# Second MoE of a fused attention kernel: GpSimd's part of the middle pass, the first rounding, the pace of the weights' decode and the place of y's first sums are changed

## The chip, the cores and the metric

The kernel runs on one core of one Trainium2 chip. The metric is the device time of one launch in microseconds. Lower is better.

## What is computed

Attention with a cumulative-decay bias over 4 x 8 heads of 576 tokens, then two mixture-like dense layers ("MoE") on the 2304 tokens, all in float32:

```python
x = attention(q, k, v, s)                      # (2304, 512)
h = np.maximum(x @ w_in, 0.0); y = h * h @ w_out          # first MoE, 512 -> 2048 -> 512
h = y @ w_in2; g = h * np.cos(h); out = g @ w_out2        # second MoE, the same sizes
```

The change touches the second MoE alone: `g = h * cos(h)` between two products, and what prepares their operands.

## The kernel before, in words

**Precision.** TensorE multiplies float16 in the second MoE. So that float32 accuracy is kept, every operand is split into a high part (rounded to float16) and a low part (the rest), and each product is three matmuls: high x high, low x high, high x low (PASSES).

**Tiling.** The tokens are cut into five blocks j (four of 512 tokens and a last one of 256), the 2048 hidden columns into 16 chunks f of 128. The order of the work is a list of items, written out in `items`: three passes over the chunks, GROUPS = (0..3), (4..8), (9..15); within a pass, all five blocks; within a block, all chunks of the pass. Items 0 to 19 are the first pass (p = 0), items 20 to 44 the middle pass (p = 1), of which items 40 to 44 are the half-size block. In the last pass (p = 2) chunks 10 to 15 of the four large blocks go two at a time, in "units".

**One item** (the loop from L1660). `m2_g1` is the first product, 12 matmuls into the PSUM tile `hp`. `m2_cos` scales it on ScalarE (`a`, L1437) and, on VectorE, rounds it to a whole number by adding and subtracting MAGIC (`kf`, L1438) and takes the difference (L1439). `m2_sin` is ScalarE's Sin (L1444). `m2_mul` multiplies by h on VectorE (L1450). `m2_high` makes the high part `gh` on ScalarE (L1458), `m2_rest` the low part `gl` (L1465): on GpSimd in the middle pass, on VectorE otherwise. `gh` and `gl` of an item are made during the next item. `m2_g2` is the second product (L1480), issued two items late (G2LAG). After the last chunk of a pass its four accumulators (two in the half-size block) leave PSUM: in the first pass they are written to `part`, in later passes added to it, alternately by VectorE (L1487) and by ScalarE and GpSimd (`os` L1492, L1493). Each engine runs its instructions in the order in which they are written.

**The decode of the weights** runs beside the items. A weight tile comes as raw 64-bit words. `w_clip` (ScalarE, L807) and `w_bits` (VectorE, L813 and L817) turn it into float32; `w_square` (ScalarE, L892) and a matmul (L901) sum its squares; `w_scale` makes a power of two of that (VectorE, L908 to L913, and `group` once for a pass); `w_rest` makes the high part (ScalarE, L840 or L866), `w_lo` the low part (VectorE, L883 or L874). How many tiles have had their bits done behind item i is the number `goal` (L1699). Tiles become ready in twos. For chunks 10 to 15 the first product's weights of two chunks are combined ("split" weights): the first of two makes four sums on VectorE (L855) and three parts, the second two parts.

**The transform of y.** In a unit the two chunks' first products are computed in seven smaller products (`prod`, Strassen-like, L1571) on sums of weights and on sums of y. `t_make` makes the sums of y for a block: its first step loads two tiles `yr` (SP's queue, L1057), then come four subtractions (VectorE, L1517), four high parts (ScalarE, L1520) and four low parts (VectorE, L1523), in six more steps. `t_tick` runs one step; it is called once behind each item from T_FROM on, and twice in each unit. The `yr` buffers (two) are also used for the sums of split weights.

**A unit** writes its products into three PSUM tiles `bank`; `snap` (ScalarE, L1581) and `join` (VectorE, L1585) bring them out into `hs`, and a later product into the same bank waits for its snap or join. Between the products stand the halves of earlier second products (`out_part`). At its end: half a second product, a step of `t_tick`, then `m2_cos` of the two chunks.

Of the kernel before, what the change touches and what calls it, by code (L numbers as in the profile page):

```python
# [13 lines left out]
ACTF = mybir.ActivationFunctionType  # L14
# [9 lines left out]
NF = DFF // 128  # L24
# [5 lines left out]
TINY = 2.0 ** -96  # L30
GROUPS = ((0, 4), (4, 9), (9, 16))
PAIR0 = 10
T_FROM = 36
RAWS = 6
NB2 = 5
LAG = (3, 5)
# [92 lines left out]
def attention_moe_moe_kernel(  # L129
# [1102 lines left out]
    def w_rest(j):  # L1232
        w_hi(j)
        wlow.append(j)
# [30 lines left out]
    def w_step(n):  # L1265

        js = list(range(nw[2], min(nw[2] + n, wlim[0])))
        while wlow:
            w_lo(wlow.pop(0))
            yield  # L1270
        w_squares()
        while wrest:
            w_rest(wrest.pop(0))
        if js:
            w_clip_to(js[-1])
            for _ in zip(*[w_bits(j) for j in js]):
                yield
            for j in js:
                if wq[j][0] == 0:
                    wrest.append(j)  # L1280
                else:
                    wbit.append(j)
            nw[2] += len(js)
# [145 lines left out]
                m += 1  # L1429
        hd2[j, f] = hp  # L1430

    def m2_cos(j, f):
        n = blocks[j][1]
        hp = hd2[j, f]
        a = p2.tile([128, n], F32, tag="a", bufs=2, name="a")
        kf = p2.tile([128, n], F32, tag="kf", bufs=2, name="kf")
        nc.scalar.activation(out=a, in_=hp, func=ACTF.Copy, scale=sm["hsc"][:, j, f:f + 1], bias=0.25)  # L1437
        nc.vector.tensor_scalar(out=kf, in0=a, scalar1=MAGIC, scalar2=MAGIC, op0=ALU.add, op1=ALU.subtract)  # L1438
        nc.vector.tensor_tensor(out=kf, in0=kf, in1=a, op=ALU.subtract)  # L1439
        hd2[j, f] = (hp, a, kf)  # L1440
# [20 lines left out]
    def m2_rest(p, j, f):  # L1461
        n = blocks[j][1]
        a, gh = hd2[j, f]
        gl = p2.tile([128, n], F16, tag="gl", bufs=3, name="gl")
        (nc.gpsimd if p == 1 else nc.vector).tensor_tensor(out=gl, in0=a, in1=gh, op=ALU.subtract)  # L1465
        hd2[j, f] = (gh, gl)

    def m2_g2(p, j, f, pick=None):
        t0, n = blocks[j]
        gh, gl = hd2[j, f]  # L1470
        w = wt[1, f, 1]
        first, last = (f == x for x in (GROUPS[p][0], GROUPS[p][1] - 1))
        sc = sm["osc"][:, p, j:j + 1]
        if first:
            ops.setdefault(j, {})
        for a in range(n // 128) if pick is None else pick:
            if first:
                ops[j][a] = ps2.tile([128, DM], F32, tag=f"o{a}", name=f"o{a}")
            for m, (e, x) in enumerate(PASSES):
                nc.tensor.matmul(  # L1480
                    ops[j][a], (gh, gl)[e][:, a * 128:(a + 1) * 128], w[:, x, :],
                    start=(first and m == 0), stop=(last and m == 2),
                )
            if last:
                st = part[4 * j + a]
                if p and (a % 2 == 0 or j == NB2 - 1):
                    nc.vector.scalar_tensor_tensor(  # L1487
                        out=st, in0=ops[j][a], scalar=sc, in1=st, op0=ALU.mult, op1=ALU.add
                    )
                elif p:  # L1490
                    os = p2.tile([128, DM], F32, tag="os", bufs=2, name="os")
                    nc.scalar.activation(out=os, in_=ops[j][a], func=ACTF.Copy, scale=sc)  # L1492
                    nc.gpsimd.tensor_tensor(out=st, in0=os, in1=st, op=ALU.add)  # L1493
                elif a % 2 == 0:
                    nc.scalar.activation(out=st, in_=ops[j][a], func=ACTF.Copy, scale=sc)
                else:
                    nc.vector.tensor_scalar(out=st, in0=ops[j][a], scalar1=sc, scalar2=None, op0=ALU.mult)
            if f == NF - 1:
                for row, x, m in _pieces(t0 + a * 128, 128):
                    nc.sync.dma_start(out=out[row:row + m, :], in_=part[4 * j + a][x:x + m])  # L1500
# [5 lines left out]
    def t_make(j):  # L1506

        to = [half[4 * (j % 2) + x].bitcast(F16).rearrange("p (e c h) -> p e c h", e=2, c=2) for x in range(4)]
        ysc = sm["ysc"][:, j:j + 1]
        load_ys(j)  # L1510
        yield
        r, q = (yr[j, a] for a in range(2))
        t3 = part[18].rearrange("p (c h) -> p c h", c=2)
        src = (r[:, 0:2], q[:, 2:4], t3, r[:, 2:4])

        def minus(o, x, y):
            nc.vector.tensor_tensor(out=o, in0=x, in1=y, op=ALU.subtract)  # L1517

        def high(x):
            nc.scalar.activation(out=to[x][:, 0], in_=src[x], func=ACTF.Copy, scale=ysc)  # L1520

        def low(x):
            nc.vector.scalar_tensor_tensor(  # L1523
                out=to[x][:, 1], in0=src[x], scalar=ysc, in1=to[x][:, 0], op0=ALU.mult, op1=ALU.subtract
            )

        minus(src[2], q[:, 2:4], q[:, 0:2])
        yield
        high(2)
        minus(src[0], q[:, 0:2], r[:, 0:2])  # L1530
        yield
        high(0)
        low(2)
        minus(src[1], q[:, 2:4], src[0])
        yield
        high(1)
        low(0)
        minus(src[3], r[:, 2:4], src[1])
        yield
        high(3)  # L1540
        low(1)
        yield
        low(3)
        yt[j] = to
# [3 lines left out]
    def t_tick(j):  # L1548

        while now2[0] <= min(j, NB2 - 2):  # L1550
            if next(now2[1], now2) is not now2:
                return
            now2[0] += 1
            now2[1] = t_make(now2[0])
# [8 lines left out]
    def prod(j, f, x, b, start):  # L1563
        m, wx, yx = PROD[x]
        w = pair[f][m]
        if start:
            bank[b] = ps2h.tile([128, 2 * HB], F32, tag="h", bufs=3, name="bank")
        n = 0
        for c in range(2):
            for a, e in PASSES:  # L1570
                nc.tensor.matmul(  # L1571
                    bank[b][:, 0:HB], w[:, a, wx, c * 128:(c + 1) * 128], y_side(j, yx, e, c),
                    start=(start and n == 0), stop=(n == 5), skip_group_check=True,
                )
                n += 1
# [13 lines left out]
    def out_part(x, n):  # L1589
        if x is not None:  # L1590
            k = blocks[x[1]][1] // 128 // 2
            m2_g2(*x, pick=range(n * k, n * k + k))

    def unit(j, f, prev):

        p = len(GROUPS) - 1
        w_need(2 * NF + 2 * f + 4)
        while now2[0] <= j:
            t_tick(j)
        first = fifo.pop(0) if len(fifo) != 2 or prev[0] != "u" else None  # L1600
        second = fifo.pop(0) if len(fifo) > 1 else None
        for m in range(2):
            hd2[j, f + m] = stq[0][0].tile([128, 2 * HB], F32, tag="stg", bufs=4, name="hs")
        old = [prev[1:], (prev[1], prev[2], prev[3] + 1)] if prev[0] == "u" else []
        prod(j, f, 1, 0, True)
        prod(j, f, 2, 1, True)
        snap(j, f, 0, 0, 0)
        join(j, f, 1, 0, 0)
        out_part(first, 0)
        for x in old:  # L1610
            m2_sin(*x[1:])
        if old:
            m2_mul(*old[0])
        else:
            m2_high(*prev[1:])
            m2_rest(*prev[1:])
        prod(j, f, 6, 0, False)
        if old:
            m2_high(*old[0])
            m2_mul(*old[1])  # L1620
        snap(j, f, 0, 1, 0)
        prod(j, f, 7, 2, True)
        out_part(first, 1)
        if old:
            m2_high(*old[1])
            m2_rest(*old[0])
            m2_rest(*old[1])
        prod(j, f, 5, 0, False)
        snap(j, f, 0, 1, 1)
        join(j, f, 2, 1, 1)  # L1630
        out_part(second, 0)
        t_tick(j + 1)
        prod(j, f, 3, 0, False)
        snap(j, f, 0, 0, 1)
        prod(j, f, 4, 2, False)
        join(j, f, 2, 1, 0)
        out_part(second, 1)
        t_tick(j + 1)
        for m in range(2):
            m2_cos(j, f + m)  # L1640
            fifo.append((p, j, f + m))

    def unit_rest(p, j, f):
        fs = (f, f + 1)
# [15 lines left out]
    for i, (kind, p, j, f) in enumerate(items):  # L1660
# [11 lines left out]
        m2_g1(j, f)  # L1672
        if prev and prev[0] == "u":
            unit_rest(*prev[1:])
        m2_cos(j, f)
        if i < G2LAG:
            m2_sin(j, f)
            m2_mul(p, j, f)
# [4 lines left out]
        if i >= QUIET:  # L1683
            w_squares()
            while wrest:
                w_rest(wrest.pop(0))
        if p == 0 and j + 2 < NB2 and f == 3:
            first_y(j + 2)
        if i >= G2LAG:
# [6 lines left out]
            last_y(j + 1)  # L1696
        w_lows()
        k = i + 1 - QUIET
        goal = min(4 * NF, bits0 + int(max(0, min(k, PAUSE)) * P_BITS) + max(0, k - PAUSE - 5))  # L1699
        if i >= QUIET:  # L1700
            _weave(w_step(max(0, goal - nw[2])))
        if i >= G2LAG:
# [66 lines left out]
```

## Time and profile before

| | us |
|---|---|
| three runs: median (lowest, highest) | 983.01 (981.57, 983.53) |
| the profiled execution | 983.83 |
| its span, first to last instruction | 982.0 |
| busy in the span: TensorE / VectorE / ScalarE / GpSimd | 951.3 / 762.3 / 687.9 / 162.2 |

The page gives TensorE (PE) 97% of the span, VectorE (DVE) 78%, ScalarE (ACT) 70%, GpSimd (POOL) 17%. It cuts the span in 40 equal slices; a digit is the busy share in tenths:

```
PE   6999999999999999999999999999999899999998
DVE  6899987778777777777994375888789987787675
POOL 2000012111110111111110032420233331001001
```

The second MoE begins near 598 us, in the 25th slice. A matmul is pipelined: the next one starts before the modelled end of the one before, so the time from start to start is the pace, and a row's duration is longer.

### The profile page before, as it was taken

The numbers are of one execution on the slowest core, as the hardware profiler recorded it, in microseconds if no ns is written. First come the engines' busy times: TensorE is split into PE (matmuls) and PEld (weight loads), VectorE is DVE, ScalarE is ACT, GpSimd is POOL, SyncE is SP. The second block draws the span as 40 slices with busy tenths as digits, with TensorE's granted clock in tenths as the row PEclk, the third lists the DMA queues.
The fourth block names the chain that finished last, engine by engine and source line by source line (L and its number), as shares of the span: only waits on it lengthen the run. The fifth ranks groups of instructions, "written<-read, shape, count | busy, mean of one in ns | idle before, by whom it ended". The sixth has DMA issues, their size and how long they took to land.

```text
span 982.0 us, 20976 instructions
## 1 busy us (share of the span) xinstructions
PE 951.3 (97%) x7472; PEld 755.7 (77%) x7472; DVE 762.3 (78%) x1905; ACT 687.9 (70%) x1669; POOL 162.2 (17%) x251
## 2 busy tenths in 40 slices
PE   6999999999999999999999999999999899999998
PEld 5898899999999999999999995445444345656664
DVE  6899987778777777777994375888789987787675
ACT  6799877778778777776784785677567655565553
POOL 2000012111110111111110032420233331001001
PEclk9999999999999999999999999999999999999999
DMA  8984698658988865587994697200000001121001
GB/s 251 301 279 135 151 221 214 168 139 177 170 187 177 184 177 156 128 160 161 200 227 90 238 323 297 64 2 1 1 1 3 21 22 44 51 77 45 27 18 65
DMA packets 151673, 131.43 MB, mean 134 GB/s; under 512 B 107992, under 2 KB 125728, under 8 KB 151568
## 3 DMA queue, kind: packets, MB, share of 16 engines
q1 hardware_dynamic: 147664, 123.78, 48.7%
q0 software_dynamic: 3904, 6.30, 2.5%
q8 instruction: 59, 0.97, 0.4%
q14 instruction: 46, 0.38, 0.1%
HBM read 89.98 MB, written 15.83 MB: 108 GB/s over the span
## 4 chain that ended last, share of the span: by engine, by line
PE 74%; DVE 10%; DMA 7%; ACT 5%; issue 3%; POOL 1%; SPq 0%; DVEq 0%; ACTq 0%; POOLq 0%
PE y L1017 18%; PE hps L988 18%; PE o L1480 14%; PE hp L1426 9%; DMA rw<-in_w_dram 6%; PE bank L1571 5%; PE qkp L560 5%; PE pvs L687 4%; DVE kf L1439 1%; DVE a L1450 1%; PE xps L742 1%; DVE kf L1438 1%; DVE st L817 1%; DVE wt L874 1%; DVE wt L880 1%
## 5 line engine op out<-in xcount | busy, mean ns | idle before, releaser
L988 PE MATMUL hps<-xh,wt 128*128 128x256 f32 x1152 | 238.6, 290 | 2.2 <-ACT g L999 2.0
L1017 PE MATMUL y<-gh,wt 128*128 128x256 f32 x1152 | 236.4, 289 | 0.0
L988 PEld LDWEIGHTS hps<-xh,wt 128*128 128x128 f32 x1152 | 189.9, 192 | 4.5 <-ACT g L999 3.5
L1017 PEld LDWEIGHTS y<-gh,wt 128*128 128x128 f32 x1152 | 189.0, 191 | 1.0
L1480 PE MATMUL o<-wt,gh 128*128 128x512 f16 x576 | 172.3, 381 | 3.7 <-ACT gh L1458 1.6
L988 PE MATMUL hps<-xl,wt 128*128 128x256 f32 x576 | 163.4, 284 | 0.2 <-DVE xl L759 0.2
L1017 PE MATMUL y<-gl,wt 128*128 128x256 f32 x576 | 163.0, 283 | 0.1
L999 ACT ACTIVATE g<-hps 128x256 f32<-128x256 f32 x144 | 54.6, 379 | 102.2 <-PE hps L988 98.0
L1426 PE MATMUL hp<-yh,wt 128*128 128x512 f16 (+1 forms) x448 | 125.2, 349 | 0.0
L1480 PE MATMUL o<-wt,gl 128*128 128x512 f16 x288 | 109.9, 382 | 3.4 <-POOL gl L1465 3.4
L988 PEld LDWEIGHTS hps<-xl,wt 128*128 128x128 f32 x576 | 110.7, 192 | 0.7 <-DVE xl L759 0.4
L1017 PEld LDWEIGHTS y<-gl,wt 128*128 128x128 f32 x576 | 110.2, 191 | 1.0 <-DVE gl L1007 0.4
L1426 PEld LDWEIGHTS <-wt 128*128 128x128 f16 x672 | 64.2, 98 | 59.6 <-issue 1.0
L1480 PEld LDWEIGHTS <-gh 128*128 128x128 f16 x576 | 56.2, 98 | 59.4 <-issue 3.5
L386 POOL DMA_DIRECT2D k<-ext_d x80 | 41.1, 514 | 322.2 <-ACT g L1000 104.6
L601 ACT ACTIVATE sb<-sb,nb 128x128 f32<-128x128 f32 (+7 forms) x152 | 87.5, 576 | 2.5 <-DVE nb L578 2.0
L1444 ACT ACTIVATE a<-kf 128x512 f32<-128x512 f32 (+1 forms) x80 | 46.7, 585 | 49.9 <-DVE kf L1439 48.9
L1007 DVE TENSOR_TENSOR gl<-g,gh 128x256 fp32r<-128x256 f32 x144 | 60.2, 418 | 27.0 <-ACT gh L1001 14.0
L1426 PE MATMUL hp<-yl,wt 128*128 128x512 f16 (+1 forms) x224 | 78.2, 349 | 0.0
L578 DVE CUSTOM_DVE_ANT_0 sb<-qkp,mask 128x128 f32<-128x128 f32 (+7 forms) x152 | 69.3, 456 | 6.9 <-PE qkp L545 3.6
L642 DVE TENSOR_SCALAR p<-sb 128x384 f16<-128x384 f32 (+3 forms) x120 | 43.2, 360 | 39.5 <-ACT sb L601 21.2
L646 DVE SCALAR_TENSOR_TENSOR p<-sb,p 128x384 f16<-128x384 f32 (+3 forms) x120 | 66.4, 553 | 3.8 <-DVE p L642 0.2
(145 smaller groups left out, 1881.9 us busy)
## 6 DMA issues: line engine op xcount, KB each, us to landing
rw<-in_w_dram SPq DMA_DIRECT2D x64, 512.0 KB
raw<-in_qk_dram SPq DMA_DIRECT2D x48, 352.0 KB
yr<-y_d SPq DMA_DIRECT2D x17, 512.0 KB
raw<-in_qk_dram SPq DMA_DIRECT2D x16, 384.0 KB
v_d<-vt SPq DMA_DIRECT2D x16, 320.0 KB
vb<-v_d SPq DMA_DIRECT2D x32, 160.0 KB
vr<-in_v_dram POOLq DMA_DIRECT2D x15, 320.0 KB, 4.6
y_d<-yst SPq DMA_DIRECT2D x18, 256.0 KB
```

Source lines behind the costliest of these rows:

```text
L560: nc.tensor.matmul(p[0:r, 0:cn], m[0:kk, qo:qo + r], m[0:kk, BT + c0:BT + c0 + cn], start=(kk == 128 and not (two and h % 2)), stop=(kk == ...
L578: nc.vector.tensor_tensor_reduce(out=sb[0:r, c0:c0 + cn], in0=p[0:r, 0:cn], in1=mask[0:r, mo:mo + cn], scale=-0.125, scalar=(3.0e38 if k = ...
L601: nc.scalar.activation(out=sb[0:r, 0:w], in_=sb[0:r, 0:w], func=ACTF.Exp, scale=-1.0, bias=j["nb"], accum_out=z[0:r, ti, x:x + 1],)
L646: nc.vector.scalar_tensor_tensor(out=p[0:r, cw:cw + w], in0=sb[0:r, 0:w], scalar=PSC, in1=p[0:r, 0:w], op0=ALU.mult, op1=ALU.subtract,)
L988: nc.tensor.matmul(hp, w[:, a, c * 128:(c + 1) * 128], (xh, xl)[e][:, c, :], start=(n == 0), stop=(n == 3 * KD - 1),)
L999: nc.scalar.activation(out=g, in_=hp, func=ACTF.Relu)
L1007: nc.vector.tensor_tensor(out=gl, in0=g, in1=gh, op=ALU.subtract)
L1017: nc.tensor.matmul(yps[k][d // 2][:, d % 2, :], w[:, a, d * 128:(d + 1) * 128], (gh, gl)[e], start=(f == 0 and n == 0 and d % 2 == 0), sto ...
L1426: nc.tensor.matmul(hp, chunk_of(w, a, c), (yh, yl)[e][:, c, :], start=(m == 0), stop=(m == 3 * KD - 1),)
L1444: nc.scalar.activation(out=a, in_=kf, func=ACTF.Sin, scale=-6.2831850)
L1480: nc.tensor.matmul(ops[j][a], (gh, gl)[e][:, a * 128:(a + 1) * 128], w[:, x, :], start=(first and m == 0), stop=(last and m == 2),)
L1571: nc.tensor.matmul(bank[b][:, 0:HB], w[:, a, wx, c * 128:(c + 1) * 128], y_side(j, yx, e, c), start=(start and n == 0), stop=(n == 5), ski ...
```

## The change

T_FROM falls from 36 to 20, and a rate LATE_BITS of 0.62 weights per item comes into `goal`: the bits of 14 weights fall behind items 19 to 40, where they fell behind items 22 to 35. At most one split weight is finished per item. In the middle pass, `gl` is made by VectorE; all accumulators leave through VectorE (L1487's form); the first rounding, adding MAGIC, is done by ScalarE as a Copy with a bias, and VectorE does both subtractions in one scalar_tensor_tensor. In a unit that follows a unit, the second step of `t_tick` stands before the fifth of the seven products and not at the end, and `m2_cos` of the two chunks stands before the last half of a second product. A unit that follows an item has one step instead of two. `t3`, a temporary of `t_make`, lies in another tile.

```diff
--- before.py
+++ after.py
@@ -30,7 +30,8 @@
 TINY = 2.0 ** -96
 GROUPS = ((0, 4), (4, 9), (9, 16))
 PAIR0 = 10
-T_FROM = 36
+T_FROM = 20
+LATE_BITS = 0.62
 RAWS = 6
 NB2 = 5
 LAG = (3, 5)
@@ -1269,7 +1270,7 @@
             w_lo(wlow.pop(0))
             yield
         w_squares()
-        while wrest:
+        while wrest and not split(wrest[0]):
             w_rest(wrest.pop(0))
         if js:
             w_clip_to(js[-1])
@@ -1429,12 +1430,19 @@
                 m += 1
         hd2[j, f] = hp
 
-    def m2_cos(j, f):
+    def m2_cos(j, f, p=2):
         n = blocks[j][1]
         hp = hd2[j, f]
         a = p2.tile([128, n], F32, tag="a", bufs=2, name="a")
         kf = p2.tile([128, n], F32, tag="kf", bufs=2, name="kf")
         nc.scalar.activation(out=a, in_=hp, func=ACTF.Copy, scale=sm["hsc"][:, j, f:f + 1], bias=0.25)
+        if p == 1:
+            nc.scalar.activation(out=kf, in_=a, func=ACTF.Copy, bias=MAGIC)
+            nc.vector.scalar_tensor_tensor(
+                out=kf, in0=kf, scalar=MAGIC, in1=a, op0=ALU.subtract, op1=ALU.subtract
+            )
+            hd2[j, f] = (hp, a, kf)
+            return
         nc.vector.tensor_scalar(out=kf, in0=a, scalar1=MAGIC, scalar2=MAGIC, op0=ALU.add, op1=ALU.subtract)
         nc.vector.tensor_tensor(out=kf, in0=kf, in1=a, op=ALU.subtract)
         hd2[j, f] = (hp, a, kf)
@@ -1462,7 +1470,7 @@
         n = blocks[j][1]
         a, gh = hd2[j, f]
         gl = p2.tile([128, n], F16, tag="gl", bufs=3, name="gl")
-        (nc.gpsimd if p == 1 else nc.vector).tensor_tensor(out=gl, in0=a, in1=gh, op=ALU.subtract)
+        nc.vector.tensor_tensor(out=gl, in0=a, in1=gh, op=ALU.subtract)
         hd2[j, f] = (gh, gl)
 
     def m2_g2(p, j, f, pick=None):
@@ -1483,7 +1491,7 @@
                 )
             if last:
                 st = part[4 * j + a]
-                if p and (a % 2 == 0 or j == NB2 - 1):
+                if p == 1 or p and (a % 2 == 0 or j == NB2 - 1):
                     nc.vector.scalar_tensor_tensor(
                         out=st, in0=ops[j][a], scalar=sc, in1=st, op0=ALU.mult, op1=ALU.add
                     )
@@ -1510,7 +1518,7 @@
         load_ys(j)
         yield
         r, q = (yr[j, a] for a in range(2))
-        t3 = part[18].rearrange("p (c h) -> p c h", c=2)
+        t3 = half[8 if j else 4].rearrange("p (c h) -> p c h", c=2)
         src = (r[:, 0:2], q[:, 2:4], t3, r[:, 2:4])
 
         def minus(o, x, y):
@@ -1625,6 +1633,7 @@
             m2_high(*old[1])
             m2_rest(*old[0])
             m2_rest(*old[1])
+            t_tick(j + 1)
         prod(j, f, 5, 0, False)
         snap(j, f, 0, 1, 1)
         join(j, f, 2, 1, 1)
@@ -1634,11 +1643,10 @@
         snap(j, f, 0, 0, 1)
         prod(j, f, 4, 2, False)
         join(j, f, 2, 1, 0)
-        out_part(second, 1)
-        t_tick(j + 1)
         for m in range(2):
             m2_cos(j, f + m)
             fifo.append((p, j, f + m))
+        out_part(second, 1)
 
     def unit_rest(p, j, f):
         fs = (f, f + 1)
@@ -1672,7 +1680,7 @@
         m2_g1(j, f)
         if prev and prev[0] == "u":
             unit_rest(*prev[1:])
-        m2_cos(j, f)
+        m2_cos(j, f, p)
         if i < G2LAG:
             m2_sin(j, f)
             m2_mul(p, j, f)
@@ -1683,7 +1691,10 @@
         if i >= QUIET:
             w_squares()
             while wrest:
-                w_rest(wrest.pop(0))
+                x = wrest.pop(0)
+                w_rest(x)
+                if split(x):
+                    break
         if p == 0 and j + 2 < NB2 and f == 3:
             first_y(j + 2)
         if i >= G2LAG:
@@ -1696,7 +1707,7 @@
             last_y(j + 1)
         w_lows()
         k = i + 1 - QUIET
-        goal = min(4 * NF, bits0 + int(max(0, min(k, PAUSE)) * P_BITS) + max(0, k - PAUSE - 5))
+        goal = min(4 * NF, bits0 + int(max(0, min(k, PAUSE)) * P_BITS) + int(max(0, k - PAUSE - 1) * LATE_BITS))
         if i >= QUIET:
             _weave(w_step(max(0, goal - nw[2])))
         if i >= G2LAG:
```

## Rows read from the trace of the kernel before

**Rows 1.** Windows: each engine's busy time in three stretches, granted clock, DMA share, GB/s.

```profile
598.00:687.26 89.26, 89.26 (x449) 42.91 (x448) 73.79 (x142) 61.22 (x117) 21.57 (x17) 1.00 0.17 60
687.26:814.89 127.63, 120.55 (x592) 55.97 (x590) 111.73 (x191) 78.99 (x152) 42.90 (x31) 0.99 0.05 14
814.89:952.10 137.21, 133.99 (x866) 84.47 (x865) 101.20 (x178) 78.81 (x150) 8.95 (x8) 1.00 0.12 42
```

**Rows 2.** Waits of PE, 687.26 to 814.89: us in total, times, longest.

```profile
PE o L1480 <- POOL gl L1465: 3.4, 4, 0.9
```

**Rows 3.** Chain of work, in order: start, us, what.

```profile
675.51 2.59 PE o L1480 x12
...
685.97 1.29 PE o L1480 x6
687.26 2.59 PE hp L1426 x12
...
812.28 1.31 PE hp L1426 x12
...
814.89 2.60 PE hp L1426 x12
```

**Rows 4.** Groups by line and shape, VectorE, 687.26 to 814.89: busy, mean ns.

```profile
L1439 DVE TENSOR_TENSOR kf<-kf,a 128x512 f32<-128x512 f32 x20 | 18.2, 912 | 0.7
...
L813 DVE TENSOR_SCALAR st<-st 128x512 int32<-128x512 int32 x14 | 13.8, 985 | 1.0 <-ACT st L807 0.8
...
L1487 DVE SCALAR_TENSOR_TENSOR wt<-o,osc,wt 128x512 f32<-128x512 f32 x8 | 5.6, 743 | 0.0
```

**Rows 5.** Timeline from 735.79: start, us, engine, line.

```profile
735.79 1.01 DVE L874 SCALAR_TENSOR_TENSOR wt<-sums,wsc,wt 128x768 f16<-128x768 f32 x1
...
737.11 0.42 DVE L813 TENSOR_SCALAR st<-st 128x512 int32<-128x512 int32 x1
...
737.56 0.69 DVE L817 SCALAR_TENSOR_TENSOR st<-rw,st 128x512 int32<-128x512 int32 x1
...
738.17 0.74 DVE L1450 SCALAR_TENSOR_TENSOR a<-hp,gsc,a 128x512 f32<-128x512 f32 x1
...
738.83 0.42 DVE L1438 TENSOR_SCALAR kf<-a 128x512 f32<-128x512 f32 x1
...
739.29 0.69 DVE L1439 TENSOR_TENSOR kf<-kf,a 128x512 f32<-128x512 f32 x1
...
739.65 1.34 POOL L1465 TENSOR_TENSOR gl<-a,gh 128x512 f16<-128x512 f32 x1 [7.25 <-ACT gh L1458]
739.90 1.38 DVE L813 TENSOR_SCALAR st<-st 128x512 int32<-128x512 int32 x1
```

**Rows 6.** Groups by line and shape, second MoE: busy, mean ns.

```profile
L1465 DVE TENSOR_TENSOR gl<-a,gh 128x512 f16<-128x512 f32 x44 | 30.3, 688 | 4.2 <-ACT gh L1458 2.8
```

**Rows 7.** Waits, 816 to 982: us in total, times, longest.

```profile
PE bank L1571 <- ACT hs L1581: 3.2, 7, 1.0
```

**Rows 8.** Timeline of the pair units, 824 to 867.

```profile
824.11 0.27 PE L1571 MATMUL bank<-yh,wt 128*128 128x256 f16 x1 [0.46 <-ACT hs L1581]
...
860.24 0.69 ACT L1492 ACTIVATE os<-o,osc 128x512 f32<-128x512 f32 x1 [1.58 <-PE o L1480]
...
860.83 0.71 ACT L1520 ACTIVATE wt<-wt,ysc 128x512 f16<-128x512 f32 x1
...
861.44 1.32 ACT L1437 ACTIVATE a<-hs,hsc 128x512 f32<-128x512 f32 x2
...
862.67 0.35 ACT L1581 COPY hs<-bank 128x256 f32<-128x256 f32 x1
863.07 1.47 PE L1571 MATMUL bank<-wt,wt 128*128 128x256 f16 x12 [0.26 <-ACT hs L1581]
...
863.43 0.63 ACT L1444 ACTIVATE a<-kf 128x512 f32<-128x512 f32 x1 [0.41 <-DVE kf L1439]
...
866.37 0.82 PE L1571 MATMUL bank<-wt,wt 128*128 128x256 f16 x6 [0.53 <-ACT hs L1581]
```

## The prediction

> **What bounds the kernel now.** I read the page first, where TensorE's slices are nearly full, so only its few gaps can be won. Cut by stage, it has no gap in the first pass of the second MoE; in the middle pass (items 20 to 44, from 687.26 to 814.89) it is busy 120.55 of 127.63 us and VectorE 111.73, and in the pair stretch behind it 133.99 of 137.21 [rows 1]. The grouped waits name the largest cause in each: in the middle pass a second matmul waits for `gl`, which GpSimd makes, and in the pair stretch the products wait for ScalarE's `snap` [rows 2, 7].
>
> The real loss is larger than the idle time, because matmuls overlap. The chain gives TensorE's own pace: 12 matmuls of a first product take 2.60 us, or 1.31 for the half-size block; of a second product 2.59, or 1.29 [rows 3]. The middle pass issues 20 full and 5 half first products, and 20 full and 5 half second products (they run two items late): 20 x 2.60 + 5 x 1.31 + 20 x 2.59 + 5 x 1.29 = 116.8 us. It takes 127.6. [...]
>
> VectorE is what is late, and two things make it so. Its operations stretch beside GpSimd: the shift L813 takes 0.42 us at 737.11 and 1.38 at 739.90, under a GpSimd `gl` of 1.34 [rows 5]. Over the middle pass L813 averages 0.985 x14 and L1439 0.912 x20 [rows 4], against 0.42 and 0.69 alone [rows 5]: 7.9 + 4.4 = 12.3 us, without the smaller groups. And its work is bunched: where a pair of halved weights falls due, both weights' sums and low parts run in one item.
>
> **The change, part by part.**
>
> GpSimd leaves the middle pass. VectorE gains 20 full `gl` at 0.688 [rows 6] and 5 half ones (about 0.42, an estimate: half the columns at a little more than half the time), 15.9 us, and 8 accumulations at 0.743 [rows 4], 5.9 us. It loses the 12.3 us of stretching.
>
> The first rounding goes to ScalarE: VectorE loses 20 x 0.42 plus 5 halves at 0.28 (estimated the same way), 9.8 us. ScalarE gains 25 operations that the trace lacks. They lie between the Sin at 0.63 and the scaling from SBUF, 1.32 for two, in steps of 0.66 [rows 8]; I take 0.63, some 14.5 us, less the 8 accumulation copies that leave it. ScalarE has the room: 78.99 us of 127.63 busy [rows 1]. The double subtraction that stays on VectorE has the shape of L817, 0.69 alone [rows 5], which is what L1439 took; at L1487's 0.743 [rows 4] it would cost 1 us more in all.
>
> [...] VectorE's rounding takes 0.42 [rows 5], ScalarE's would take 0.63. [...]
>
> Is the chain too long then? From the end of item i's first product to its second product, TensorE does four products, 10.4 us. The chain in that time: scale and rounding on ScalarE, subtraction 0.69, Sin 0.63, multiply 0.74, some 3.8 us with hand-offs; then, queued behind the next item's scale and rounding (which end 6.5 us after), the high part 0.6 and `gl` 0.69: about 8 us. **2.4 us of slack** in a full item, about none in a half one (its window is 5.2).
>
> The decode is spread: 14 weights between items 19 and 40 instead of 22 and 35. I sum VectorE per item in steps (start to start, alone: L813 0.45, L817 0.61, L1450 and other scalar-tensor-tensor 0.66, L1439 and `gl` 0.61) [rows 5]. Base of a full item: 0.61 + 0.66 + 0.61 = 1.9 against 5.2 of TensorE. Bits of one weight 1.06; low parts of two plain weights 1.3; scales 0.5; four accumulations 2.6. A pair's first weight: four sums of 256 columns (an estimate: 0.4 each, L1438's 0.42 for 512 columns [rows 5] as the upper bound), 1.5 in steps, and its low parts 1.5, together 2.9; its second one 1.3, most of it the 768-column piece of 1.01 [rows 5]. With the transform's earlier start (T_FROM 20, one subtraction and one low part per item from 21 to 26, 5.1 in all) the heaviest items are 24 (6.1), 26 (6.2) and 27 (6.4); 25 has 2.5 and 28 3.2. The backlog peaks at 2.2 us behind item 27, inside the slack: no stall. Early loading also frees the transform from the buffers that it shared with the pair sums, and takes its work out of the crowded end.
>
> The end of the pass is different. Items 40 to 44 are the half-size block: TensorE needs 5 x 1.31 + 2 x 2.59 + 3 x 1.29 = 15.6 us. VectorE has there: item 40 first weight of the last pair, bits and scale, 5.9; item 41 second weight and four accumulations, 5.1; item 42 1.1; item 43 low parts, scales and the group's tables (some 1.5), 4.5; item 44 1.1: 17.7 us. Followed in order, the multiply of item 41 stands behind the accumulations and the pair's low parts, and its second product starts about 1.8 us late; that of item 42 about 0.5 late behind the tables. With hand-offs of 0.1 each I take **2.8 us** left in the middle pass. Bounds: 0.3 if the queue drains between the products, 6.6 if neither backlog (3.1 behind item 41, 3.5 behind 43) finds slack.
>
> The pair units. Seven waits for a snap cost 3.2 us idle [rows 7], and each another 0.16 of lost overlap (matmuls of 0.27 start 0.11 apart): 4.3. The first unit's two, some 0.6 with the 0.46 at 824.11 [rows 8], have another cause: there is no other work to put between. The other five follow one pattern: at 860.24 ScalarE copies the last accumulation (it had to wait for TensorE), then runs the transform's 0.71, then two scalings, 1.32, and only at 862.67 the snap for which the product at 863.07 waits [rows 8]; the second wait of such a unit comes from the same late start of the roundings (0.53 at 866.37). In the change the two scalings stand ahead of the accumulation, and the transform's second step in mid-unit: 2.0 us (0.71 + 1.32) are done before 860.24, while ScalarE sat idle, against delays of about 0.4 and 0.7 a snap (0.26 and 0.53 idle, and 0.16 each). So 2.6 + 5 x 0.16 = **3.4 us** go. The accumulations on VectorE now stand behind four rounding operations (2.1 us); their PSUM bank is next written after two products, half a second product and two more products, 3.9 us of TensorE, so that hides. The transform's step in mid-unit adds 1.3 us to VectorE ahead of a join; the roundings ahead of it now start over a microsecond earlier, which covers it. In each block one tick fewer comes before the next block: its last low part and the load behind it move into the single item between units. SP's queue holds nothing else that is due, but the load lands later and the next subtraction waits for it in VectorE's queue; I charge 0.5 for the two blocks with one, between 0 and the 3.4 of this part. First unit: its rounding no longer meets a GpSimd `gl`; 0.3 gained, 0.6 stays.
>
> **Sum**, against the profiled execution (983.83 us, span 982.0 and 1.8 around it): 10.8 - 2.8 + 3.4 - 0.5 + 0.3 = 11.2 less, 972.6. The median of the runs is 983.01, 0.8 below that execution; on it **971.8**.
>
> **Rivals.**
> [...]
> - *The pair units keep their waits*, as the moved transform step or its late load takes the scalings' place in the queue. For it: VectorE stands in order. Against: ScalarE alone was late at 860 to 863 [rows 8]. 971.8 + 3.4 - 0.5 = 974.7, and 975.2 if the late load is paid as well.
> - *The chain bounds, not VectorE's queue.* Then ScalarE's rounding adds 0.2 in each of 25 items: 5 us, 976.8. Against: TensorE loses nothing where items are light and GpSimd still makes `gl`. [...]
> - *Slower: VectorE's long operations are not GpSimd's doing.* If they stay, VectorE has 111.7 + 15.9 + 5.9 - 9.8 = 123.7 us; with the 15.9 idle that it showed, the pass takes 139.6 instead of 127.6, less 3.2 from the pairs: 8.8 more, 991.8. It decides once less than 8.8 us of stretching go, of the 12.3 counted above. Against it stands the pair 0.42 and 1.38 of one operation [rows 5].
> - *Better: nothing is left of the stalls* but the first unit's 0.6, if VectorE drains in time at the half-size block too: 983.0 - (10.8 + 4.3 - 0.6) = 968.5. That GpSimd stays in the middle pass is no rival: its two uses there are both replaced, and those that stay in the last pass stand in no wait of the middle one.
>
> **Chances.** Forecast 0.60; half-size block 0.14; pair units 0.11; chain 0.03; better, to 968.5, 0.05; slower 0.04; 0.03 for mishaps that leave it within 0.2% (2.0 us, what a measurement can tell here from no change). Adding a little to the last two for what I did not see: faster 0.91, same 0.04, slower 0.05. The range runs from 968.5 to 977.0, which takes in the first three rivals.
>
> **What the changed profile would show.** No GpSimd instruction between 687 and 806; L813 at 0.42 throughout; a middle pass of about 119 us, what is left of its waits in the last 16 us; the five snap waits at the unit starts gone; the first unit's wait of 0.46 still there. I am wrong if VectorE's operations still stretch in the middle pass, if TensorE stalls around items 26 to 28, or if waits for VectorE's joins appear in the units.

## The result and the profile after

The changed kernel takes 971.81 us (median; 970.91 to 972.02 in four runs), against 982.31 for the kernel before in the same set of runs: a ratio of 0.989, 95% interval 0.9873 to 0.9907. Its profiled execution took 970.91 us with a span of 969.1.

The chain of waits of the changed kernel (start, us, what) gives the two ends of the middle pass, as [rows 3] did before. Lines move by a few numbers: the first product is now L1427, the second L1488.

```profile
684.57 1.30 PE o L1488 x6
685.87 2.59 PE hp L1427 x12
...
802.49 1.31 PE hp L1427 x12
803.79 1.45 PE o L1488 x6
805.24 2.59 PE hp L1427 x12
```

Item 20 begins at 685.87 and item 45 at 805.24: the middle pass takes 119.37 us where it took 127.63. The windows of the changed kernel, from the first matmul of item 20 to that of item 45 and from there to the end (length, then busy time of PE, weight loads, DVE, ACT, POOL; granted clock, DMA share, GB/s), answer to [rows 1]:

```profile
685.70:805.08 119.38, 117.83 (x592) 55.88 (x591) 98.63 (x199) 87.49 (x169) 0.00 (x0) 1.00 0.03 10
805.08:969.10 164.02, 159.53 (x1027) 100.25 (x1025) 122.22 (x218) 92.05 (x177) 10.11 (x8) 1.00 0.12 43
```

POOL has nothing to do in the middle pass, the mean granted clock there is 1.00 instead of 0.99, and VectorE is busy 98.63 us though it took over GpSimd's work. The rest takes 164.0 us, where it took 167.3 in the kernel before (row "before" of the table below). So 8.2 us come from the middle pass and 3.3 from the rest. The profiled executions differ by 12.9 us. The other 1.4 lie ahead of item 20, where both kernels do the same: in thirteen other profiles of this study that first part ended between 686.2 and 687.8, so 685.7 is an early one. That part is not the change's.

VectorE's and ScalarE's groups by shape in the middle pass of the changed kernel (busy us, mean ns, idle before), with the rows that answer to [rows 4] and [rows 6]:

```profile
L1441 DVE SCALAR_TENSOR_TENSOR kf<-kf,a 128x512 f32<-128x512 f32 x20 | 13.8, 690 | 16.1 <-ACT kf L1440 15.9
L1473 DVE TENSOR_TENSOR gl<-a,gh 128x512 f16<-128x512 f32 x20 | 13.7, 684 | 0.1
L1495 DVE SCALAR_TENSOR_TENSOR wt<-o,osc,wt 128x512 f32<-128x512 f32 x16 | 10.9, 743 | 0.0
...
L814 DVE TENSOR_SCALAR st<-st 128x512 int32<-128x512 int32 x14 | 5.9, 419 | 0.0
```

```profile
L1440 ACT ACTIVATE kf<-a 128x512 f32<-128x512 f32 x20 | 12.6, 630 | 0.6
```

The shift is back at 0.419 us from 0.985, the double subtraction takes 0.690, ScalarE's rounding 0.630. What TensorE still waits for, from item 20 to the end (us in total, times, longest):

```profile
PE o L1488 <- ACT gh L1466: 1.3, 1, 1.3
PE bank L1579 <- ACT hs L1589: 0.5, 1, 0.5
PE o L1488 <- DVE wt L1495: 0.2, 1, 0.2
```

The timeline shows the largest of them, in the half-size block. Four accumulations stand in VectorE's queue, then the low parts of the last split weight, and only then the multiply of item 41, whose high part the second product at 800.99 needs:

```profile
796.06 2.72 DVE L1495 SCALAR_TENSOR_TENSOR wt<-o,osc,wt 128x512 f32<-128x512 f32 x4
796.86 0.59 PE L1488 MATMUL o<-wt,gh 128*128 128x512 f16 x2 [0.18 <-DVE wt L1495]
...
798.70 1.01 DVE L875 SCALAR_TENSOR_TENSOR wt<-sums,wsc,wt 128x768 f16<-128x768 f32 x1
799.62 0.48 DVE L875 SCALAR_TENSOR_TENSOR wt<-st,wsc,wt 128x256 f16<-128x256 f32 x1
800.02 0.48 DVE L1458 SCALAR_TENSOR_TENSOR a<-hp,gsc,a 128x256 f32<-128x256 f32 x1
...
800.53 0.40 ACT L1466 CAST gh<-a 128x256 f16<-128x256 f32 x1 [1.88 <-DVE a L1458]
...
800.99 0.60 PE L1488 MATMUL o<-wt,gh 128*128 128x512 f16 x2 [1.33 <-ACT gh L1466]
```

In the pair units the place of [rows 8] now looks like this, on ScalarE: both scalings lie ahead of the last accumulation copy, and the snap follows that copy at once.

```profile
848.59 1.43 ACT L1438 ACTIVATE a<-hs,hsc 128x512 f32<-128x512 f32 x2
850.14 0.69 ACT L1500 ACTIVATE os<-o,osc 128x512 f32<-128x512 f32 x1
850.79 0.37 ACT L1589 COPY hs<-bank 128x256 f32<-128x256 f32 x1
```

### The profile page after: what moved, and what is told of

It reads as the page before. It is cut to its first block, busy times and chain, and to the rows that moved or that the text cites. A ratio compares the mean times of both kernels' runs of the same rounds, so it can differ in the third digit from the quotient of the medians.

```text
span 969.1 us, 20903 instructions
## 1 busy us (share of the span) xinstructions
PE 947.4 (98%) x7472; PEld 755.4 (78%) x7472; DVE 752.1 (78%) x1913; ACT 697.9 (72%) x1686; POOL 117.8 (12%) x218
## 4 chain that ended last, share of the span: by engine, by line
PE 84%; DVE 6%; ACT 6%; issue 1%; DMA 1%; POOL 1%; SPq 0%; DVEq 0%; ACTq 0%; POOLq 0%
PE hps L989 19%; PE y L1018 18%; PE o L1488 18%; PE hp L1427 12%; PE bank L1579 5%; PE qkp L561 5%; PE pvs L688 4%; DMA rw<-in_w_dram 1%; PE xps L743 1%; ACT sb L602 1%; ACT wt L835 1%; DVE wt L881 1%; ACT st L808 1%; DVE sb L579 1%; DVE wt L1495 1%
## 5 line engine op out<-in xcount | busy, mean ns | idle before, releaser
L1488 PE MATMUL o<-wt,gh 128*128 128x512 f16 x576 | 171.3, 379 | 1.5 <-ACT gh L1466 1.3
L1427 PE MATMUL hp<-yh,wt 128*128 128x512 f16 (+1 forms) x448 | 124.9, 348 | 0.0
L1427 PEld LDWEIGHTS <-wt 128*128 128x128 f16 x672 | 64.0, 98 | 59.1
L1488 PE MATMUL o<-wt,gl 128*128 128x512 f16 x288 | 109.2, 379 | 0.0
L1488 PEld LDWEIGHTS <-gh 128*128 128x128 f16 x576 | 56.3, 98 | 56.3 <-ACT gh L1466 1.6
L1427 PE MATMUL hp<-yl,wt 128*128 128x512 f16 (+1 forms) x224 | 78.0, 348 | 0.0
```

The source lines that it names most:

```text
L1427: nc.tensor.matmul(hp, chunk_of(w, a, c), (yh, yl)[e][:, c, :], start=(m == 0), stop=(m == 3 * KD - 1),)
L1488: nc.tensor.matmul(ops[j][a], (gh, gl)[e][:, a * 128:(a + 1) * 128], w[:, x, :], start=(first and m == 0), stop=(last and m == 2),)
```

## The experiments

The theory on trial: in the middle pass VectorE's in-order queue is late, because its operations stretch beside GpSimd and because its work comes in bunches; in the pair units ScalarE's order makes the snaps late. Rivals: the long operations are not GpSimd's doing; the chain of one item bounds; each part of the change removes a cause of its own. All ratios are against the kernel before on the same chip (median 982.6 to 982.9 in these sets).

Each kernel's middle pass and rest come from the windows of its one profiled execution. The length and the busy times of DVE and POOL are the columns to read; the text in front of the fences names the kernels. Stages that kernels share repeat to about 0.1 us: the middle pass takes 127.62 in both the kernel before and a_units, and the rest between 164.02 and 164.11 in the changed kernel, u_round, u_spread, late66, late70 and paced.

### One part of the change alone

`a_gpsimd`: low parts and all accumulations of the middle pass on VectorE.

```diff
-        (nc.gpsimd if p == 1 else nc.vector).tensor_tensor(out=gl, in0=a, in1=gh, op=ALU.subtract)
+        nc.vector.tensor_tensor(out=gl, in0=a, in1=gh, op=ALU.subtract)
-                if p and (a % 2 == 0 or j == NB2 - 1):
+                if p == 1 or p and (a % 2 == 0 or j == NB2 - 1):
```

> The kernel before with one part alone: in the middle pass GpSimd is replaced by VectorE (low parts and accumulations), all else as before. My theory (VectorE's queue is late because its operations stretch beside GpSimd, and because its work is bunched): the stretching goes, L813 back at 0.42 us throughout, but the bunches at each pair of split weights stay and VectorE has 21.8 us more of its own: about 5 of the 10.8 us of the middle pass go, 976 to 979 against 982.5. Rival (the long operations are not GpSimd's doing): L813 still near 1 us on average and the kernel slower than before, 990 or more. Rival (the chain of one item bounds): a shorter low part (0.69 instead of 1.6) saves 0.9 in every item, so most of the 10.8 us go, 973.

`a_round`: the change's `m2_cos` with its call, nothing else.

> The kernel before with one part alone: the first rounding of the middle pass on ScalarE. My theory: VectorE loses 9.8 us of its work, and the double subtraction still stretches beside GpSimd: 2 to 5 us go, 978 to 980.5 against 982.5. Rival (the chain of one item bounds, so a 0.63 us operation in place of a 0.42 one only lengthens it): 3 to 5 us slower, 986.

`a_units`: in `unit`, the moved `t_tick` and `m2_cos`, nothing else.

> The kernel before with one part alone: in the pair units the transform's second step in mid-unit and the two scalings before the last half product. My theory: the middle pass as before, the five waits for a snap at the starts of units gone, 2.9 to 3.4 us less: 979.3. Rival (the moved step takes the scalings' place in the queue): waits for a snap or a join stay, less than 1 us gained, 981.7 or more.

`a_spread`: T_FROM, LATE_BITS, one split weight per item, and `t3`, nothing else.

> The kernel before with one part alone: the decode at 0.62 weights per item, one split weight per item, the transform of y from item 20 on. My theory (two causes, stretching and bunching): the bunches go, the stretching stays, 3 to 6 us of the 10.8 go: 976.5 to 979.5. Rival (stretching alone is the cause): the sum of VectorE's work is unchanged, so less than 1 us goes, 981.5 or more. Rival (bunching alone is the cause): about 8 us go, 974.5.

Measured medians: a_gpsimd 977.67 (ratio 0.9948, 0.9936 to 0.9961), a_round 978.21 (0.9956, 0.9944 to 0.9968), a_units 980.48 (0.9977, 0.9968 to 0.9986), a_spread 977.42 (0.9946, 0.9934 to 0.9959). Windows of the kernel before, middle pass and rest, and then of the middle pass in the order a_gpsimd, a_round, a_spread:

```profile
687.10:814.72 127.62, 120.53 (x591) 55.97 (x590) 111.89 (x192) 78.98 (x151) 42.90 (x31) 0.99 0.05 14
814.72:982.00 167.28, 160.17 (x1027) 100.17 (x1025) 119.02 (x216) 91.10 (x178) 11.45 (x10) 1.00 0.13 44
```

```profile
687.65:809.01 121.36, 118.69 (x591) 55.47 (x590) 108.76 (x226) 74.84 (x145) 0.00 (x0) 1.00 0.05 16
```

```profile
687.78:809.70 121.92, 118.48 (x592) 55.69 (x591) 97.94 (x170) 93.11 (x178) 38.49 (x31) 1.00 0.06 18
```

```profile
686.18:807.17 120.99, 117.97 (x591) 56.04 (x590) 106.29 (x191) 79.27 (x151) 41.53 (x31) 1.00 0.03 10
```

and of a_units, middle pass and rest:

```profile
686.68:814.30 127.62, 120.54 (x592) 55.97 (x590) 111.86 (x192) 79.01 (x151) 42.92 (x31) 0.99 0.05 14
814.30:978.70 164.40, 159.69 (x1027) 100.27 (x1025) 121.94 (x216) 92.47 (x178) 11.46 (x10) 1.00 0.13 45
```

| middle pass / rest, us | middle | rest | L813 or its like, mean us |
|---|---|---|---|
| before | 127.62 | 167.28 | 0.985 |
| a_gpsimd | 121.36 | 166.89 | 0.420 |
| a_round | 121.92 | 167.20 | 0.837 |
| a_spread | 120.99 | 167.23 | 0.644 |
| a_units | 127.62 | 164.40 | 0.985 |
| the whole change | 119.38 | 164.02 | 0.419 |

The unit order works on the rest alone, 2.9 us, as expected. The other three work on the middle pass, and each by about six: 6.3, 5.7 and 6.6 us, 18.6 together where the whole change gains 8.2. a_gpsimd also takes 0.4 us off the rest: the first unit there waits once and not twice (6 waits for a snap instead of 7). By medians the gains are smaller, 5.0, 4.5 and 5.3 us and 2.2 for a_units (979.3 was expected, 980.48 came); the profiled execution of the kernel before, 983.83, lies 1.1 above the median of 982.7 here, and in which stage that lies is not shown. The proportions stay.

So the three are largely substitutes: three ways to let late work come up in time. Part of the overlap is one loss that all three remove. In the kernel before, TensorE runs at about half its pace for some 3.4 us, right behind two waits (start, us):

```profile
762.64 0.60 PE L1480 MATMUL o<-wt,gh 128*128 128x512 f16 x2 [0.98 <-ACT gh L1458]
...
764.06 0.39 PE L1480 MATMUL o<-wt,gl 128*128 128x512 f16 x1 [0.82 <-POOL gl L1465]
...
766.30 1.06 PE L1480 MATMUL o<-wt,gh 128*128 128x512 f16 x2
767.16 0.63 PE L1480 MATMUL o<-wt,gl 128*128 128x512 f16 x1
767.58 0.64 PE L1426 MATMUL hp<-yh,wt 128*128 128x512 f16 x1
```

Matmuls there start 0.43 us apart, where 0.215 is the pace elsewhere, and the granted clock from 766 to 768 is 0.50; from 764.72 to 768.35 that costs about 1.7 us (an estimate from these starts). The granted clock of the middle pass is 1.00 in a_gpsimd, a_round and a_spread, so each of them counts this loss as its own.

That fells the chain rival, by which ScalarE's slower rounding costs time and a shorter `gl` wins nearly everything, and the rival that GpSimd has nothing to do with the long operations: with POOL at 0.00 the shift takes 0.420 us at once.

### GpSimd's stretching by itself

`dummy` is the changed kernel, and GpSimd makes the low part once more, for nobody.

```diff
         nc.vector.tensor_tensor(out=gl, in0=a, in1=gh, op=ALU.subtract)
+        if p == 1:
+            jk = p2.tile([128, n], F16, tag="jk", bufs=1, name="jk")
+            nc.gpsimd.tensor_tensor(out=jk, in0=a, in1=gh, op=ALU.subtract)
```

> The changed kernel, and in the middle pass GpSimd makes the low part once more, into a tile that nobody reads; VectorE makes the one that is used. It measures the stretching by itself, without anything waiting for GpSimd's result (only the buffers of a and gh come free a little later). My theory: VectorE's operations stretch again (L813's form from 0.42 to 0.8 us or more on average, the double subtraction likewise), VectorE's sum in the middle pass grows by 8 us or more, and TensorE loses 2 to 6 us more there: 974 to 978 against 971.8. Rival (what cost time was only the wait for GpSimd's late result): no stretching that matters, 971 to 972.5.

It took 975.16 us (0.992, 0.9906 to 0.9933). Its middle pass, and four of VectorE's groups in it:

```profile
687.62:809.56 121.94, 118.22 (x591) 55.73 (x590) 111.66 (x199) 88.64 (x169) 32.76 (x23) 1.00 0.03 9
```

```profile
L1473 DVE TENSOR_TENSOR gl<-a,gh 128x512 f16<-128x512 f32 x20 | 18.5, 926 | 0.3
L1458 DVE SCALAR_TENSOR_TENSOR a<-hp,gsc,a 128x512 f32<-128x512 f32 x20 | 14.9, 745 | 1.1 <-ACT a L1452 1.1
L1441 DVE SCALAR_TENSOR_TENSOR kf<-kf,a 128x512 f32<-128x512 f32 x20 | 13.8, 688 | 6.1 <-ACT kf L1440 5.9
...
L814 DVE TENSOR_SCALAR st<-st 128x512 int32<-128x512 int32 x14 | 9.7, 692 | 0.0
```

The instructions of VectorE are the same 199; their time rises from 98.63 to 111.66 us, and the middle pass by 2.6. Two of the expectations were missed: the shift goes to 0.692 and not to 0.8 or more, and the double subtraction does not stretch at all (0.688 against 0.690). ScalarE waited three times for the extra operation to release `a`, 2.4 us in total (at 741.80, 751.72 and 772.62); TensorE's four waits in the middle pass lie at 730.73, 800.88, 805.01 and 808.69, none of them there.

`gl`, with both inputs in SBUF, goes from 0.684 to 0.926 us on average, while the multiply, one of whose inputs lies in PSUM, keeps 0.745. The double subtraction, which has two SBUF inputs too, keeps 0.688: in this trace the full-size ones that run beside a GpSimd operation begin ahead of it (or, once, in its last 0.06 us); a half-size one that begins 0.16 us behind (at 807.50) takes 0.80 instead of 0.42. The shift, with a single input, in SBUF, goes from 0.419 to 0.692. Why an operation beside GpSimd gets longer, no run shows.

### The change without one part

`u_gpsimd`, `u_round` and `u_spread` are the changed kernel with the part of that name put back.

> The changed kernel with GpSimd back in the middle pass (low parts, half of the accumulations with ScalarE's copy); rounding on ScalarE, spread decode and unit order as changed. The three parts for the middle pass removed 6.3, 5.7 and 6.6 us of it alone and 8.3 together. If they are substitutes that empty one queue, undoing one costs little: 1 to 2 us, 973 to 974. If each had its own cause, undoing this one costs 5 us: 977.

> The changed kernel with the first rounding back on VectorE (0.46 us a step in each full item). As substitutes: VectorE's heaviest items 26 and 27 rise to 6.7 and 6.9 of 5.2 us, the backlog behind item 27 to 3.5, about 1 us over the slack, and the half-size block gets worse by the same: 1.5 to 3 us more, 973.5 to 975. If each had its own cause: 4.5 us more, 976.5.

> The changed kernel with the old pace of the decode and the old place of y's transform. As substitutes: the bunched items (both split weights in one, 7.6 of 5.2 us) return but nothing stretches and the base is 0.46 lighter: 1 to 2.5 us more, 973 to 974.5. If each had its own cause: 5.3 us more, 977.

Measured: 973.07 (0.9901, 0.9887 to 0.9915), 973.03 (0.99, 0.9887 to 0.9914) and 971.79 (0.9887, 0.9873 to 0.99). Their middle passes, in that order:

```profile
687.01:806.72 119.71, 117.54 (x591) 56.06 (x590) 93.32 (x168) 91.99 (x176) 36.53 (x31) 1.00 0.03 10
```

```profile
687.01:807.34 120.33, 117.95 (x592) 55.88 (x591) 107.55 (x223) 75.23 (x144) 0.00 (x0) 1.00 0.03 10
```

```profile
686.16:805.33 119.17, 118.00 (x592) 55.76 (x591) 99.75 (x201) 88.10 (x170) 0.00 (x0) 1.00 0.06 18
```

Against 119.38 for the whole change: 0.3 more, 1.0 more, 0.2 less. The first two bear out the substitutes: each costs far less than the 5 or 4.5 us that a cause of its own would have cost. u_round's median is a little below its range. u_gpsimd's 973.07 lies in its range, but the stages give only 0.7 of the 1 to 2 us, 0.3 here and 0.4 in the rest (164.38). For the third I expected 1 to 2.5 us and got nothing: with the other parts in place the spread only moves what is lost. Without it TensorE's waits lie where the old bunches fell due, as the timeline of u_spread shows, and none in the half-size block:

```profile
759.65 0.61 PE L1487 MATMUL o<-wt,gh 128*128 128x512 f16 x2 [0.29 <-ACT gh L1465]
...
760.47 0.39 PE L1487 MATMUL o<-wt,gl 128*128 128x512 f16 x1 [0.21 <-DVE gl L1472]
...
781.64 0.60 PE L1487 MATMUL o<-wt,gh 128*128 128x512 f16 x2 [0.55 <-ACT gh L1465]
```

### Where the rest of the loss lies

Each differs from the changed kernel in the pace of the decode; `late66` and `late70` in the one constant LATE_BITS.

> The changed kernel with LATE_BITS 0.66 instead of 0.62, so that the bits end behind item 39 and the last pair's two weights fall due in items 39 and 40. By my sums of VectorE's work per item: item 39 has 6.4 of 5.2 us (in the slack), items 40 and 41 have 2.7 and 3.7 of 3.9, item 42 4.4 of 2.6, and no other bunch is made (split weights in 27 and 28, 33 and 34): the 1.5 and 0.35 us lost at 796 to 801 go, 0.3 to 0.7 us stay, 970.2 against 971.8. Rival (what is lost there is the half-size block's own chain, whose slack is nothing): the loss stays, 971.8.

> The changed kernel with LATE_BITS 0.70: the end is lighter still, but the first split weight falls due in item 26, together with four accumulations, bits and the transform's last step: 9.7 of 5.2 us, 2 us over the slack. My theory: the loss at 796 to 801 goes and one of 1.5 to 2.5 us comes at about 725 to 732: 971.8 to 972.5. Rival (the half-size block's own chain): the loss at the end stays and nothing comes in front: 971.8 with the wait in its old place.

late66 took 973.22 us (0.99, 0.9885 to 0.9914), late70 971.42 (0.9884, 0.9863 to 0.9905). TensorE's waits in the middle pass of late66:

```profile
PE o L1488 <- DVE gl L1473: 1.3, 1, 1.3
PE o L1488 <- DVE wt L1495: 0.5, 1, 0.5
PE o L1488 <- ACT gh L1466: 0.2, 1, 0.2
```

and the two of late70, in its timeline:

```profile
729.49 0.60 PE L1488 MATMUL o<-wt,gh 128*128 128x512 f16 x2 [0.31 <-ACT gh L1466]
...
730.70 0.39 PE L1488 MATMUL o<-wt,gl 128*128 128x512 f16 x1 [0.61 <-DVE gl L1473]
```

late66 was a miss: I let 1.8 us of backlog stand in item 42, in a block to which the prediction itself gave no slack. There the pass's scales and tables (thirteen small operations from 800.87 on in its trace) stand ahead of item 42's `gl`, and the wait only changed its cause. late70 did what was expected, in a smaller size: the end is clear and about 0.9 us of waiting appears at 729 (1.5 to 2.5 were expected), where split weight, accumulations and transform meet. So a list that keeps them apart was tried, `paced`, and with it `paced_unit`, which puts something behind the fifth product of the first unit.

```diff
-LATE_BITS = 0.62
+BITS_AT = (19, 21, 22, 24, 25, 27, 28, 29, 30, 32, 33, 34, 35, 36)
...
-        goal = min(4 * NF, bits0 + int(max(0, min(k, PAUSE)) * P_BITS) + int(max(0, k - PAUSE - 1) * LATE_BITS))
+        goal = min(4 * NF, bits0 + int(max(0, min(k, PAUSE)) * P_BITS) + sum(i >= x for x in BITS_AT))
```

```diff
-        out_part(first, 1)
+        if second is not None:
+            out_part(first, 1)
...
         join(j, f, 2, 1, 1)
+        if second is None:
+            out_part(first, 1)
         out_part(second, 0)
```

> The changed kernel with the items behind which bits fall written out (19, 21, 22, 24, 25, 27, 28, 29, 30, 32, 33, 34, 35, 36), so that split weights fall due in 27 and 28, 32 and 33, 37 and 38, never in an item with accumulations (26, 31, 36, 41), and the pass's tables in item 39: nothing of the decode meets the half-size block. My theory (what is left is bunching in VectorE's queue, and its place is set by the items in which the decode falls due): no item is more than 1.2 us over its share, the middle pass takes 117.0 to 117.6 us instead of 119.4, 969.5 to 970.2 against 971.8. Rival (the half-size block's own chain): 0.5 to 1.5 us stay lost there, 971.

> The kernel before this one in the list, and in a unit without a second second product the last half of the first one stands behind the fifth small product, so that something lies between it and the next one that waits for its snap. My theory: the first unit's wait of 0.46 goes, 0.4 to 0.6 us less than the list kernel, 969.0 to 969.8. Rival (the snap in front of the fifth product is late instead): the wait moves to the fifth product, no gain.

paced took 970.72 us (0.9875, 0.9859 to 0.9892), paced_unit 969.72 (0.9869, 0.9855 to 0.9884). The middle pass of paced, then middle pass and rest of paced_unit:

```profile
687.77:804.90 117.13, 117.13 (x592) 56.24 (x591) 100.09 (x201) 87.95 (x170) 0.00 (x0) 1.00 0.03 10
```

```profile
687.83:804.97 117.14, 117.14 (x592) 56.25 (x591) 100.11 (x201) 87.95 (x170) 0.00 (x0) 1.00 0.03 10
804.97:968.40 163.43, 159.36 (x1027) 100.28 (x1025) 121.22 (x216) 91.71 (x176) 10.12 (x8) 1.00 0.13 43
```

TensorE is busy in the whole middle pass, and 117.13 us is its own pace. That is the stage that was expected for paced; its median, 970.72, lies above the range and nearer to the rival's 971, so that the stage decides and not the whole time. The half-size block has no loss of its own: what was lost there was the decode's tail. The first unit's wait went too, for 0.7 us of the rest (164.10 in paced). Against the changed kernel the two stages of paced_unit are 2.2 and 0.6 us shorter; as whole times the intervals of the two ratios overlap, so that much is shown by the stages and not by the medians. Against the kernel before it is clearly faster, by the most of all.

## Why the prediction was right

The forecast was 971.8, the measurement 971.81. The closeness is partly luck. The forecast took 11.2 us off a median of 983.01; by the medians of one set the gain is 10.5 (982.31 to 971.81). And the first part of the kernel, up to item 20, moves by more than a microsecond from one execution to the next (it ended between 685.7 and 687.8 in the profiles). The stages are the test.

- **The middle pass.** Forecast 10.8 lost (127.6 less a pace of 116.8) and 2.8 left, 8.0 gained; measured 8.2. The pace of 116.8 was 0.3 short of the 117.13 that paced shows; by that pace 10.5 were lost and 2.2 are left. The wait for item 41's second product was put at 1.8 us and is 1.33 of idle time; item 42's at 0.5, where the second product of 803.79 takes 1.45 instead of 1.29. The hand-offs of 0.1 in that sum were the author's estimate; ahead of the wait of 1.33 they are 0.03 and 0.06 (from VectorE to ScalarE at 800.53, from there to TensorE at 800.99). A wait of 0.18 for an accumulation at 796.86 was not forecast. Around items 26 to 28, where the heaviest backlog stayed inside the slack by the sums, no wait is listed; one matmul, at 727.92, starts 0.2 us late.
- **The stretching.** Shown: 0.985 to 0.419 with POOL empty, and back up to 0.692 in `dummy`. Its size was put too low. The prediction counted 12.3 us in the two largest groups; compared group by group, the kernel before with the changed one, it comes to some 22. Among those left out is the half-size rounding, 0.880 us in the kernel before and 0.284 in u_round, five times. By the prediction's own terms VectorE would have 111.7 + 15.9 + 5.9 - 12.3 - 9.8 = 111.4 us; it has 98.63. What the stretching costs TensorE is another matter. Where the other parts are in place, GpSimd's return adds 0.3 us to the middle pass: it stretches VectorE's operations again, and it takes so many off VectorE that the sum still falls by 5.3 us (98.63 to 93.32). TensorE's two waits there are new ones, 1.36 us for ScalarE's accumulation copy and 0.81 for GpSimd's `gl`; why they come to nearly the same total as those of the changed kernel is not shown.
- **Rounding on ScalarE.** 0.630 and 0.690 as sized. The rounding takes 0.21 us longer there than the 0.42 of [rows 5] on VectorE, and a_round alone still gains 5.7 us in the middle pass: VectorE, whose queue was late, is busy 97.94 us in it instead of 111.89.
- **The spread.** The prediction gave the other two parts a price in VectorE's time and this one none. Alone it gains 6.6 us, in the change nothing (u_spread): the rows show waits at 759 to 782 without it and at 796 to 801 with it, so the pace of 0.62 carries the bunch from the middle of the pass into its end.
- **The pair units.** Forecast 3.4 - 0.5 + 0.3 = 3.2, measured 3.3. The total holds and one term does not: the 0.5 was charged for a late load and was paid, at about 0.7, for late snaps. No subtraction waits for the late load: at 847.64 it starts without a gap. What stays is a late snap in three of the units: in the first of them the product that needs it starts at 855.34, 0.41 us behind the matmul of 854.93, where 0.22 is the pace; the other two lose 0.26 each. The same three stay in a_units, so they come with the unit order. The first unit's wait of 0.46 is still there, as forecast, at 814.15. The prediction did not look for the cause of the late snaps. The accumulations that GpSimd keeps in the last pass now fall on the roundings, and one of them stretches, to 1.77 us where the one at 849.89 takes 0.69; timeline of the changed kernel:

```profile
850.90 1.27 POOL L1501 TENSOR_TENSOR wt<-os,wt 128x512 f32<-128x512 f32 x1 [1.33 <-ACT os L1500]
850.95 1.77 DVE L1447 TENSOR_TENSOR kf<-kf,a 128x512 f32<-128x512 f32 x1
...
852.81 0.63 ACT L1452 ACTIVATE a<-kf 128x512 f32<-128x512 f32 x1 [1.12 <-DVE kf L1447]
```

That this stretched rounding makes those three snaps late is read from the order of the rows; no run took the accumulation away there.

- **The slower rival** needed less than 8.8 us of stretching to go; it all went, and dummy shows whose it was. The half-size block, with 0.14 in the chances and inside the range like the pair units and the chain, was the right place, and its upper bound of 6.6 us the wrong size: about 2 us stay there, and the granted clock of the middle pass is 1.00.

## What to carry to other kernels

Where one in-order engine makes the bounding engine wait, add up its work per step of the program, not per stage: VectorE was busy 88% of the middle pass before and 85% in `paced`, with 10.5 us of TensorE's time lost in the one and none in the other. Parts that relieve the same queue are not additive: measure each alone and each taken out before calling one of them the cause. A pace constant is best chosen against the list of the other due events, above all where the steps become shorter.

## What the runs showed of the hardware

GpSimd operations whose result nobody needs, 23 of them, cost 13 us of VectorE's time in 122 (98.63 to 111.66 for the same 199 instructions). In these rows of two traces the operation that begins second is the one that gets longer: in `dummy` a `gl` that begins 0.19 us behind GpSimd's operation takes 1.65 us (at 744.42), one that begins just ahead of it takes its usual 0.69 (at 740.07), and GpSimd's then takes 1.69, where the shortest full-size one takes 1.16. In the kernel before, the difference L1439 at 743.50, 0.11 us behind a GpSimd `gl`, takes 1.60 and that `gl` 1.16; the one at 739.29, 0.36 ahead, takes 0.69 and the `gl` 1.34. Taking work from GpSimd to VectorE made VectorE's sum smaller, 111.89 to 108.76 in a_gpsimd, with 34 instructions more.
